# The last layer's output product: split into f16 halves instead of four-byte ones, with g scaled by a power of two

## Chip, cores and metric

The kernel runs on one core of a Trainium2 chip. The metric is the device time of one execution in microseconds (us): 507.54 us is the median of three runs before the change (507.1 to 508.44).

## What is computed

Attention with sigmoid weights, a soft mixture of experts, and a last layer on its output:

```python
scores = q @ k.T / sqrt(64) - log(448)               # 4 batches x 12 heads, 448 tokens, head size 64
x = (sigmoid(scores) @ v) -> (1792, 768)
x = moe(x, phi, w1, w2)                              # 32 slots, 8 experts
h = x @ w_in                                         # 768 -> 2048
g = h * cos(h)
out = g @ w_out                                      # 2048 -> 768
```

The mixture ends in a product with 32 slots, so the kernel folds it into the last layer: m = slot_out @ w_in has 32 rows only, and h is the product of m and the tokens' combine weights.

## The kernel before

The change lies in the last layer, from about 250 us on. The 1792 tokens are four blocks t of 448, d_ff = 2048 is 16 chunks f of 128, and the 768 outputs are 6 tiles o of 128. A **unit** u is a pair (t, f). For each unit TensorE makes h (`hidden`, L1199: one product of 128x128 and 128x448); ScalarE and VectorE make g = h cos(h) from it in five passes of 448 elements (`scaled`, `rounded`, `centred`, `sined`, `product`, L1177 to L1193); and TensorE adds w_out[f].T @ g to six accumulators (`out_tile`, L1234). There are eight accumulation banks: six hold the accumulators of the current block, two the h of the units to come. A **stretch** is a run of units of one block; at its end the six accumulators are emptied (`evict`, L1256 to L1262) into SBUF, and either go out or are added to a later stretch of that block.

The first four units (`PLAIN`) multiply four-byte floats as they are, two records on TensorE for each output tile. The other sixty are **split**: `upper` (L1208, ScalarE) rounds g to fp32r as gh, `lower` (L1212, VectorE) makes gl = g - gh, and each output tile is three products, gh with wh, gh with wl, gl with wh. wh and wl are made likewise of w_out by `wo_hi` (L1120, ScalarE) and `wo_lo` (L1123, VectorE). w_out arrives as 64-bit floats in six buffers; `wo_abs` and `wo_steps` (`narrow`, L264 to L271) make 32-bit floats of a chunk, one pass on ScalarE and three on VectorE, one of them a shift (L267). A buffer is loaded again as soon as `wo_lo` has read it.

The order of the units sets when chunks are needed:

```python
SOME, PLAIN = 6, 4
units = [(t, f) for t in range(2) for f in range(SOME)] + [(2, f) for f in range(NF)]
units += [(t, f) for t in range(2) for f in range(SOME, NF)]
units += [(t, f) for t in range(3, B) for f in range(NF)]
```

The first few instructions are written by hand (`m_hi` to `out_half`). From there a planner (`Plan`, filled by `schedule`) sets the order on every engine: each step has an engine, a cost and its predecessors, TensorE's steps get their due times from the sum of the costs ahead of them, the others from who needs them, and at each moment the ready step that is due first is issued. Each engine then runs its instructions in that order. A unit's h may be made once unit u-2's product is done (two banks), and `upper` waits for the last tile of unit u-2 (two buffers for gh and gl). m itself comes from a last set of products; `m_split_lo` (L1157) finishes it, and the units from 3 on read parts of it that arrive by DMA.

Of the kernel before, what the change touches and what calls it, by code (L numbers as in the profile page):

```python
# [9 lines left out]
F16 = mybir.dt.float16  # L10
F32 = mybir.dt.float32
F32R = mybir.dt.float32r
U32 = mybir.dt.uint32
AF = mybir.ActivationFunctionType
ALU = mybir.AluOpType
AX = mybir.AxisListType
PSUM = bass.MemoryType.PSUM

B, H, S, D = 4, 12, 448, 64
HP = H // 2  # L20
NP = B * HP
NT, DM = B * S, H * D
# [3 lines left out]
P = 128  # L26
NT_B = S // 32
KD = DM // P
NF = DFF // P
# [9 lines left out]
LATE = 1  # L39

CV = 512
F64_SCALE = 2.0 ** -112

LOG2E = 1.0 / math.log(2.0)
# [114 lines left out]
def fused(ctx: ExitStack, tc: tile.TileContext, qk, vv, phi, w1, w2, w_in, w_out, out):  # L159
    nc = tc.nc  # L160
# [6 lines left out]
    ident = const.tile([P, P], F32, name="ident")  # L167
# [141 lines left out]
    with ExitStack() as at:  # L309
# [58 lines left out]
        top, bottom = rows = slice(0, D), slice(D, P)  # L368
# [311 lines left out]

        pieces = [(c, n) for c in range(KD) for n in range(DFF // CV)]
        narrowing = {}

        def narrow_piece(p):
            c, n = pieces[p]
            k, o = divmod(n * CV, 1024)
            w = wt["wi", 0, c, k].bitcast(U32).rearrange("p a (f t) -> p (a f) t", t=2)
# [217 lines left out]
    ps_h = ctx.enter_context(reuse("ps_h", bufs=2, space=PSUM))  # L905
# [23 lines left out]
    m_ps, MC = {}, 4 * P  # L929
# [27 lines left out]
    with ExitStack() as ex:  # L957
# [3 lines left out]
        with tc.manual_schedule():  # L961
# [99 lines left out]
            for c in range(0, F // P - 2, 2):  # L1061
                w2_rows(1, c)
                if c == 0:
                    ps = [choose(0, k) for k in range(2)]
# [12 lines left out]
            ps = choose(1, 0)  # L1077
# [12 lines left out]

    wctx.close()
    wop = ctx.enter_context(reuse("wop", bufs=1, side="right"))
    wl = wop.tile([P, NF, DM], F32R, name="wl")
    wh = wop.tile([P, NF, DM], F32R, name="wh")
    more_wo.append(ctx.enter_context(reuse("more_wo", bufs=1, side="right")))
    stg = ctx.enter_context(reuse("stg", bufs=3))
    gp = ctx.enter_context(reuse("gp", bufs=2))
    m4 = places["m4"].tile([P, DFF], F32R, tag="w", name="m4")
# [3 lines left out]
    def whole(f):  # L1102

        return wo[f][:, :, 1].bitcast(F32)

    steps = {}
# [10 lines left out]
            steps[f].pop(0)()  # L1117

    def wo_hi(f):
        nc.scalar.copy(wh[:, f], whole(f))  # L1120

    def wo_lo(f):
        nc.vector.tensor_sub(wl[:, f], whole(f), wh[:, f].bitcast(F32))  # L1123
        load_wo(f + WO_SLOTS)

    def m_parts(f):
# [14 lines left out]
    mh, ml = [ring[:, (12 + k) * S:(12 + k) * S + 3 * P] for k in range(2)]  # L1141
# [16 lines left out]
        spread([0], (2, 3))  # L1158
        spread(range(1, 4), range(4))

    SOME, PLAIN = 6, 4
    units = [(t, f) for t in range(2) for f in range(SOME)] + [(2, f) for f in range(NF)]
    units += [(t, f) for t in range(2) for f in range(SOME, NF)]
    units += [(t, f) for t in range(3, B) for f in range(NF)]
    gs, acc, sums = {}, {}, {}

    spare = [raw_wo[k].rearrange("p m t -> p (m t)")[:, 2 * DM:2 * DM + S].bitcast(F32) for k in range(A_SLOTS)]

    def buf(k):
        return ring[:, k * S:(k + 1) * S]  # L1170

    hs, tmp = {}, {}
# [17 lines left out]

    def times(u, cols):
        ph, tn, g = tmp[u]
        nc.vector.tensor_mul(g[:, cols], hs[u][:, cols], tn[:, cols])  # L1193

    def hidden(u):
        t, f = units[u]
        ps = ps_h.tile([P, 512], F32, tag="h", name=f"h{u}")
        h = hs[u] = ps[:, 0:S]
        nc.tensor.matmul(h, m4[:, f * P:(f + 1) * P], ct4[:, t * S:(t + 1) * S], start=True, stop=True)  # L1199
        tmp[u] = [spare[k] if u == 0 else buf(3 * (u % 4) + k) for k in range(3)]  # L1200

    def product(u):
        times(u, whole_s)
        gs[u] = [tmp.pop(u)[2]]

    def upper(u):
        gs[u].append(gp.tile([P, S], F32R, tag="gh", name=f"gh{u}"))
        nc.scalar.copy(gs[u][1], gs[u][0])  # L1208

    def lower(u):  # L1210
        gs[u].append(gp.tile([P, S], F32R, tag="gl", name=f"gl{u}"))
        nc.vector.tensor_sub(gs[u][2], gs[u][0], gs[u][1].bitcast(F32))  # L1212

    def out_half(cols, os):

# [8 lines left out]
    def out_tile(u, o):  # L1224
        t, f = units[u]
        if begins(u):
            acc[o] = bank(o, f"o{u}_{o}")
        ps, cols = acc[o][:, 0:S], slice(o * P, (o + 1) * P)
        if u < PLAIN:
            terms = [(whole(f), gs[u][0])]  # L1230
        else:
            terms = [(wh[:, f], gs[u][1]), (wl[:, f], gs[u][1]), (wh[:, f], gs[u][2])]
        for n, (w, g) in enumerate(terms):
            nc.tensor.matmul(  # L1234
                ps, w[:, cols], g, start=begins(u) and n == 0, stop=ends(u) and n == len(terms) - 1
            )
# [7 lines left out]
    def adds(u):  # L1244
        return units[u][0] < 2 and units[u][1] == NF - 1

    def by_vector(u, o):
        return adds(u) or units[u][1] == NF - 1 and o % 2 == 1

    def evict(u, o):  # L1250
        t, f = units[u]
        ps = acc[o][:, 0:S]
        copy = nc.vector.tensor_copy if by_vector(u, o) else nc.scalar.copy
        if f < NF - 1:
            sums[t, o] = buf(18 + o) if t == 0 else buf(24 + o) if o < 3 else spare[o - 3]
            copy(sums[t, o], ps)  # L1256
            return
        res = buf(12 + o)
        if adds(u):
            nc.vector.tensor_add(res, ps, sums[t, o])  # L1260
        else:
            copy(res, ps)  # L1262
        nc.sync.dma_start(out=out[o * P:(o + 1) * P, t * S:(t + 1) * S], in_=res)

    plan = Plan()
    Op = plan.add

    def schedule():

        n_units = len(units)  # L1270
        mul, hid, tile, freed, raw_done = {}, {}, {}, {}, {}
        parts, his, los = {}, {}, {}

        def load(f):
            if f < WO_SLOTS:
                return -9.0, ()
            return -9.0, (landed[f],)

        landed = {}

        def chunk(f):
            if f in parts:
                return
            if f > 2:
                a = Op("act", .82, lambda: wo_abs(f), [landed.get(f), parts.get(f - 3)])
            else:
                a = None
            for c in (.6, 1., .9):
                a = Op("dve", c, lambda: wo_steps(f), [a])
            parts[f] = a  # L1290

        def split(f):
            if f in los:
                return
            if f > 1:
                chunk(f)
            his[f] = Op("act", .8, lambda: wo_hi(f), [parts.get(f)])
            los[f] = Op("dve", .9, lambda: wo_lo(f), [his[f], tile.get((f, NO - 1)) if f < PLAIN else None])
            if f + WO_SLOTS < NF:
                landed[f + WO_SLOTS] = Op("sp", 1.95, lambda: None, [los[f]])  # L1300

        def wave_ops(u):
            if u > 2:
                hid[u] = Op("pe", .2, lambda: hidden(u), [mul.get(u - 2), hid.get(u - 1)])
            a = Op("act", .57, lambda: scaled(u, whole_s), [hid.get(u), downs.get(u - 4) or tile.get((u - 4, NO - 1))])
            a = Op("act", .57, lambda: rounded(u, whole_s), [a])
            a = Op("dve", .54, lambda: centred(u, whole_s), [a])
            a = Op("act", .5, lambda: sined(u, whole_s), [a])
            mul[u] = Op("dve", .54, lambda: product(u), [a])
            if u >= PLAIN:  # L1310
                g = Op("act", .5, lambda: upper(u), [mul[u], tile.get((u - 2, NO - 1))])
                ups[u] = g
                downs[u] = Op("dve", .54, lambda: lower(u), [g])

        ups, downs = {}, {}

        def tiles(u, os):
            t, f = units[u]
            for o in os:
                need = [last_tile[0]]  # L1320
                if o == 0:
                    need += [mul.get(u)] if u < PLAIN else [ups[u], downs[u], his[f], los[f]]
                    need += [parts.get(f)]
                if begins(u):
                    need.append(freed.get(o))
                tile[u, o] = last_tile[0] = Op(
                    "pe", .694 if u < PLAIN else .602, lambda o=o: out_tile(u, o), need
                )
                if ends(u):
                    freed[o] = Op(  # L1330
                        "dve" if by_vector(u, o) else "act", .55, lambda o=o: evict(u, o), [tile[u, o]]
                    )

        last_tile = [None]
        wave_ops(2)
        wave_ops(3)
        for u in range(1, n_units):
            f = units[u][1]
            if u > 1:
                if u < PLAIN:  # L1340
                    chunk(f)
                else:
                    split(f)
            tiles(u, range(2))
            if u + 3 < n_units:
                wave_ops(u + 3)
            tiles(u, range(2, NO))
# [99 lines left out]
```

## Time and profile before

| | |
|---|---|
| median of three runs | 507.54 us (507.1 to 508.44) |
| span of the profiled execution | 506.7 us; the execution's own time is not shown |
| TensorE products busy | 481.8 us (95%), 4560 |
| TensorE weight loads busy | 349.3 us (69%), 4560 |
| VectorE busy | 325.5 us (64%), 655 |
| ScalarE busy | 292.3 us (58%), 508 |
| mean granted TensorE clock | 0.993 |

Busy times are averages over stages with different limits: attention runs to 150 us, the experts' weights stream in until about 245 us, and the last layer takes the rest. Matmuls are pipelined, so a record of 0.36 us does not mean that the next product starts 0.36 us later; the distance between starts is the pace.

### The profile page before, as it was taken

Reading aid. Unit: us, or ns where it says so; the run is one execution under the profiler, and the core shown is the slowest. Engines: PE = TensorE matmul, PEld = TensorE weight load, DVE = VectorE, ACT = ScalarE, POOL = GpSimd, SP = SyncE. Lnnn points to the kernel's source line nnn. Section 1 sums busy time; section 2 is a strip of 40 time slices with the busy share of each in tenths; the row PEclk is TensorE's granted clock in tenths of the full one; section 3 lists DMA queues with packets and bytes.
Section 4 is the critical chain, followed back from the end, with each engine's and each line's share of the span. In section 5 each row is a group of like instructions: output and inputs, shape, how many; then the busy total and the mean of one; then the engine's idle time right before and its main releaser. Section 6 shows DMA issues by size and latency. Waiting matters only on the chain.

```text
span 506.7 us, 11038 instructions
## 1 busy us (share of the span) xinstructions
PE 481.8 (95%) x4560; PEld 349.3 (69%) x4560; DVE 325.5 (64%) x655; ACT 292.3 (58%) x508; POOL 0.7 (0%) x7
## 2 busy tenths in 40 slices
PE   8998989999999998677999999999999999999997
PEld 5665556565565323222567999999999899899996
DVE  4898879999975063000689899996644654654442
ACT  5887858877861002000679889865655545555552
POOL 0000000000000000000000000000000000000000
PEclk9999999999999998999999999999999999999999
DMA  7999979979839999999824633000210110020003
GB/s 254 393 314 329 295 254 358 328 225 361 278 116 378 403 417 415 413 415 389 354 56 149 232 124 125 1 2 0 76 35 1 45 64 1 26 85 0 1 0 110
DMA packets 33442, 99.12 MB, mean 196 GB/s; under 512 B 3568, under 2 KB 17520, under 8 KB 33392
## 3 DMA queue, kind: packets, MB, share of 16 engines
q1 hardware_dynamic: 33392, 98.42, 53.3%
q8 instruction: 36, 0.59, 0.5%
q14 instruction: 14, 0.11, 0.1%
HBM read 92.11 MB, written 5.51 MB: 193 GB/s over the span
## 4 chain that ended last, share of the span: by engine, by line
PE 66%; DMA 18%; DVE 11%; ACT 2%; issue 2%; SPq 0%; DVEq 0%; ACTq 0%
PE o L1234 45%; DMA w<-in_w 14%; PE av L414 6%; PE sc L395 4%; DMA raw<-in_qk 3%; PE h L1199 3%; DVE lo L376 2%; PE sl L633 2%; DVE wi L268 1%; DVE hi L373 1%; PE idle L474 1%; DVE xt L424 1%; DMA wi<-in_w_in 1%; PE o L1219 1%; PE m L945 1%
## 5 line engine op out<-in xcount | busy, mean ns | idle before, releaser
L1234 PE MATMUL o<-gh,wh 128*128 128x448 f32 x360 | 132.3, 367 | 0.4 <-DVE wi L1260 0.4
L1234 PE MATMUL o<-gl,wh 128*128 128x448 f32 x360 | 131.5, 365 | 0.0
L1234 PE MATMUL o<-gh,wl 128*128 128x448 f32 x360 | 131.5, 365 | 0.0
L403 ACT ACTIVATE a<-sc,bias_s 128x896 f32<-128x896 f32 x72 | 71.1, 1006 | 27.1 <-PE sc L395 19.6
L1234 PEld LDWEIGHTS o<-gh,wh 128*128 128x128 f32 x360 | 67.6, 188 | 7.3 <-issue 1.3
L1234 PEld LDWEIGHTS o<-gh,wl 128*128 128x128 f32 x360 | 67.6, 188 | 5.4 <-issue 0.2
L1234 PEld LDWEIGHTS o<-gl,wh 128*128 128x128 f32 x360 | 67.6, 188 | 5.3
L1212 DVE TENSOR_TENSOR gl<-wi,gh 128x448 fp32r<-128x448 f32 x60 | 37.4, 623 | 41.1 <-ACT gh L1208 37.9
L1208 ACT CAST gh<-wi 128x448 fp32r<-128x448 f32 x60 | 34.1, 568 | 51.2 <-PE o L1234 49.3
L414 PE MATMUL av<-a,v 128*64 128x224 f32 x576 | 60.4, 357 | 2.6 <-DVE xt L424 1.5
L414 PEld LDWEIGHTS av<-a,v 128*64 128x64 f32 x576 | 39.0, 137 | 23.2 <-issue 4.1
L1193 DVE TENSOR_TENSOR wi<-h,wi 128x448 f32<-128x448 f32 x63 | 39.2, 622 | 21.5 <-ACT wi L1189 21.1
L1189 ACT ACTIVATE wi<-wi 128x448 f32<-128x448 f32 x63 | 36.4, 578 | 24.8 <-DVE wi L1184 24.7
L1184 DVE SCALAR_TENSOR_TENSOR wi<-wi 128x448 f32<-128x448 f32 x63 | 39.2, 622 | 15.3 <-ACT wi L1180 15.3
L1008 PE MATMUL so<-w,zone 128*32 128x256 f32 (+1 forms) x256 | 34.2, 517 | 9.8 <-DMA w<-in_w 9.8
L395 PEld LDWEIGHTS <-hi 64*64 64x64 f16 x768 | 25.0, 107 | 21.9 <-issue 13.5
L1180 ACT ACTIVATE wi<-wi 128x448 f32<-128x448 f32 x63 | 36.5, 580 | 1.7
L395 PE MATMUL sc<-hi 64*64 64x448 f16 (+1 forms) x384 | 34.0, 342 | 2.3 <-ACT a L403 1.6
L1177 ACT ACTIVATE wi<-h 128x448 f32<-128x448 f32 x63 | 33.9, 538 | 3.8 <-PE h L1199 3.6
L395 PE MATMUL sc<-hi,lo 64*64 64x448 f16 (+1 forms) x384 | 33.3, 330 | 0.0
L395 PE MATMUL sc<-lo,hi 64*64 64x448 f16 (+1 forms) x384 | 33.1, 329 | 0.1
L1008 PEld LDWEIGHTS so<-w,zone 128*32 128x32 f32 x256 | 9.7, 114 | 31.4 <-DMA w<-in_w 20.3
(160 smaller groups left out, 552.3 us busy)
## 6 DMA issues: line engine op xcount, KB each, us to landing
w<-in_w SPq DMA_DIRECT2D x28, 768.0 KB, 15.1
w<-in_w SPq DMA_DIRECT2D x30, 512.0 KB, 5.7
wi<-in_w_in SPq DMA_DIRECT2D x24, 512.0 KB, 7.3
wo<-in_w_out SPq DMA_DIRECT2D x16, 768.0 KB, 7.0
w<-in_w SPq DMA_DIRECT2D x11, 1024.0 KB, 9.5
raw<-in_qk SPq DMA_DIRECT2D x48, 224.0 KB, 5.1
v<-in_vv SPq DMA_DIRECT2D x24, 224.0 KB, 4.9
out_t<-wi SPq DMA_DIRECT2D x24, 224.0 KB, 2.0
```

The source lines that it names most:

```text
L395: nc.tensor.matmul(ps[to, j, 0:cols.stop - cols.start], keys[at, first:first + D], q[at, cols], **flags)
L403: nc.scalar.activation(a, ps, AF.Sigmoid, bias=bias_s, scale=qk_scale)
L414: nc.tensor.matmul(av[i][rows[j], k, 0:S // 2], v32[i][at, vc:vc + D], a[at, j, sides[k] if g < 3 else slice(0, S // 2)], start=g == 0, st ...
L1008: nc.tensor.matmul(e2[g, k][j * NS:(j + 1) * NS, 0:n], h1[g][:, c, j * NS:(j + 1) * NS], w(j), start=c == 0, stop=c == F // P - 1,)
L1177: nc.scalar.activation(tmp[u][0][:, cols], hs[u][:, cols], AF.Copy, bias=0.25, scale=inv2pi)
L1180: nc.scalar.activation(tmp[u][1][:, cols], tmp[u][0][:, cols], AF.Copy, bias=magic)
L1184: nc.vector.scalar_tensor_tensor(out=ph[:, cols], in0=tn[:, cols], scalar=-magic, in1=ph[:, cols], op0=ALU.add, op1=ALU.subtract)
L1189: nc.scalar.activation(tmp[u][1][:, cols], tmp[u][0][:, cols], AF.Sin, scale=-2.0 * math.pi)
L1193: nc.vector.tensor_mul(g[:, cols], hs[u][:, cols], tn[:, cols])
L1208: nc.scalar.copy(gs[u][1], gs[u][0])
L1212: nc.vector.tensor_sub(gs[u][2], gs[u][0], gs[u][1].bitcast(F32))
L1234: nc.tensor.matmul(ps, w[:, cols], g, start=begins(u) and n == 0, stop=ends(u) and n == len(terms) - 1)
```

## The change

It stores wh, wl, gh and gl in f16 instead of fp32r. So that the halves fit f16's range, w_out is multiplied by 8 as it is split, and g by a power of two, which is worked out on the chip from the largest magnitude of m (`bound`, `bound_row`, `powers`, `powers_all`, `keep_powers`: two maxima along rows and three small steps on VectorE, a product with the identity on TensorE that lays the 128 maxima into one row, five small steps on VectorE, a product that hands the two powers to all partitions, and a copy). Evictions of scaled units multiply by the inverse. The plain units stay unscaled, so block 0's first stretch now ends after them.

```diff
-    wl = wop.tile([P, NF, DM], F32R, name="wl")
-    wh = wop.tile([P, NF, DM], F32R, name="wh")
+    wl = wop.tile([P, NF, DM], F16, name="wl")
+    wh = wop.tile([P, NF, DM], F16, name="wh")
...
     def wo_hi(f):
-        nc.scalar.copy(wh[:, f], whole(f))
+        nc.scalar.activation(wh[:, f], whole(f), AF.Copy, scale=W_SCALE)
 
     def wo_lo(f):
-        nc.vector.tensor_sub(wl[:, f], whole(f), wh[:, f].bitcast(F32))
+        nc.vector.scalar_tensor_tensor(
+            out=wl[:, f], in0=whole(f), scalar=W_SCALE, in1=wh[:, f], op0=ALU.mult, op1=ALU.subtract
+        )
...
-    SOME, PLAIN = 6, 4
-    units = [(t, f) for t in range(2) for f in range(SOME)] + [(2, f) for f in range(NF)]
-    units += [(t, f) for t in range(2) for f in range(SOME, NF)]
+    SOME, PLAIN = (4, 6), 4
+    units = [(t, f) for t in range(2) for f in range(SOME[t])] + [(2, f) for f in range(NF)]
+    units += [(t, f) for t in range(2) for f in range(SOME[t], NF)]
...
     def times(u, cols):
         ph, tn, g = tmp[u]
-        nc.vector.tensor_mul(g[:, cols], hs[u][:, cols], tn[:, cols])
+        if u < PLAIN:
+            nc.vector.tensor_mul(g[:, cols], hs[u][:, cols], tn[:, cols])
+            return
+        nc.vector.scalar_tensor_tensor(
+            out=g[:, cols], in0=hs[u][:, cols], scalar=g_scale, in1=tn[:, cols], op0=ALU.mult, op1=ALU.mult
+        )
...
     def upper(u):
-        gs[u].append(gp.tile([P, S], F32R, tag="gh", name=f"gh{u}"))
+        gs[u].append(gp.tile([P, S], F16, tag="gh", name=f"gh{u}"))
...
     def lower(u):
-        gs[u].append(gp.tile([P, S], F32R, tag="gl", name=f"gl{u}"))
-        nc.vector.tensor_sub(gs[u][2], gs[u][0], gs[u][1].bitcast(F32))
+        gs[u].append(gp.tile([P, S], F16, tag="gl", name=f"gl{u}"))
+        nc.vector.tensor_sub(gs[u][2], gs[u][0], gs[u][1])
...
     def evict(u, o):
...
+        if adds(u):
+            nc.vector.scalar_tensor_tensor(
+                out=res, in0=ps, scalar=g_back, in1=sums[t, o], op0=ALU.mult, op1=ALU.add
+            )
+        elif by_vector(u, o):
+            nc.vector.tensor_scalar_mul(res, ps, g_back)
+        elif u < PLAIN:
+            nc.scalar.copy(res, ps)
+        else:
+            nc.scalar.activation(res, ps, AF.Copy, scale=g_back)
...
-                hid[u] = Op("pe", .2, lambda: hidden(u), [mul.get(u - 2), hid.get(u - 1)])
+                hid[u] = Op("pe", .2, lambda: hidden(u), [mul.get(u - 2), hid.get(u - 1), scaling.get(u)])
...
-            mul[u] = Op("dve", .54, lambda: product(u), [a])
+            mul[u] = Op("dve", .54, lambda: product(u), [a, x if u >= PLAIN else None])
...
-                    "pe", .694 if u < PLAIN else .602, lambda o=o: out_tile(u, o), need
+                    "pe", .694 if u < PLAIN else .567, lambda o=o: out_tile(u, o), need
...
+        x, scaling = None, {}
+        for eng, cost, step in (
+            ("dve", 1.2, bound), ("pe", .25, bound_row), ("dve", .6, powers), ("pe", .1, powers_all),
+            ("dve", .1, keep_powers),
+        ):
+            x = Op(eng, cost, step, [x])
+        scaling[3] = x
```

How this moves instructions shows at three places. The first is TensorE's order at unit 1, the second of the plain units (`h2` is the hidden product of unit 2, `o0_3` an accumulator of block 0's first stretch, tile 3). Before:

```order
L1199 MATMUL h2_3738<-ct4_3288,m4_3601 128x448
L1219 MATMUL o0_5_3740<-wo2_3527,wo0_3523 128x224 x2
L1199 MATMUL h3_3745<-ct4_3288,m4_3601 128x448
L1234 MATMUL o0_0_3679<-wi_64,wo1_3525 128x448
L1234 MATMUL o0_1_3681<-wi_64,wo1_3525 128x448
L1234 MATMUL o0_2_3683<-wi_64,wo1_3525 128x448
```

And in the change:

```order
L1208 MATMUL h2_3740<-ct4_3288,m4_3601 128x448
L1228 MATMUL o0_5_3742<-wo2_3527,wo0_3523 128x224 x2
L1243 MATMUL o0_0_3681<-wi_64,wo1_3525 128x448
L1294 MATMUL scale_3754<-ident_58,scales_3602 1x128
L1243 MATMUL o0_1_3683<-wi_64,wo1_3525 128x448
L1308 MATMUL scale_3754<-row_3603 128x2
L1243 MATMUL o0_2_3685<-wi_64,wo1_3525 128x448
L1208 MATMUL h3_3770<-ct4_3288,m4_3601 128x448
```

The hidden product of unit 3 has moved behind three tiles of unit 1, and the two small products stand between those tiles.

The second place is VectorE's order from the end of the split of m on (`wf2`, `wo2` are chunk 2 of w_out on its way to 32 bits). Before:

```order
L1157 TENSOR_TENSOR wi_64<-m2_3553,wi_64 128x384
L1193 TENSOR_TENSOR wi_64<-h1_3668,wi_64 128x448
L267 TENSOR_SCALAR wf2_3696<-wf2_3696 128x768
L1184 SCALAR_TENSOR_TENSOR wi_64<-wi_64 128x448
L268 SCALAR_TENSOR_TENSOR wf2_3696<-wo2_3527,wf2_3696 128x768
```

In the change, from the product of unit 1 on:

```order
L1198 TENSOR_TENSOR wi_64<-h1_3670,wi_64 128x448
L1285 TENSOR_REDUCE scales_3602<-m4_3601 128x1
L1288 TENSOR_REDUCE scales_3602<-wi_64 128x1
L1289 TENSOR_TENSOR scales_3602<-scales_3602 128x1
L1290 MEMSET row_3603 1x128
L269 TENSOR_SCALAR wf2_3698<-wf2_3698 128x768
L1299 TENSOR_REDUCE row_3603<-scale_3754 1x1
L1300 TENSOR_SCALAR row_3603<-row_3603 1x1
L1301 TENSOR_SCALAR row_3603<-row_3603 1x1
L1302 TENSOR_SCALAR row_3603<-row_3603 1x1
L1305 TENSOR_SCALAR row_3603<-row_3603 1x1
L1188 SCALAR_TENSOR_TENSOR wi_64<-wi_64 128x448
```

Nine of the ten small steps stand in a block there, with one shift of chunk 2 between them; the tenth, the copy of the powers, follows the last row.

The third place is TensorE's order where the split units begin, at unit 4. Before:

```order
L1234 MATMUL o0_5_3740<-wi_64,wo3_3604 128x448
L1234 MATMUL o0_0_3679<-gh4_3806,wh_3591 128x448
L1234 MATMUL o0_0_3679<-gh4_3806,wl_3590 128x448
L1234 MATMUL o0_0_3679<-gl4_3813,wh_3591 128x448
L1234 MATMUL o0_1_3681<-gh4_3806,wh_3591 128x448
```

In the change:

```order
L1243 MATMUL o0_5_3742<-wi_64,wo3_3606 128x448
L1243 LDWEIGHTS wh_3591
L1243 MATMUL o4_0_3835<-gh4_3818,wh_3591 128x448
L1243 LDWEIGHTS wl_3590
L1243 MATMUL o4_0_3835<-gh4_3818,wl_3590 128x448
L1243 LDWEIGHTS wh_3591
L1243 MATMUL o4_0_3835<-gl4_3827,wh_3591 128x448
```

Each weight load is now an instruction of its own (1080 more on TensorE in all), and unit 4 begins a new accumulator, since it is block 1's first.

## Rows read from the trace of the kernel before

**Rows 1.** Busy us (instructions) by stretch; then PEclk, DMA share, GB/s.

```profile
300.00:350.00 50.00, 50.00 (x249) 46.33 (x248) 45.88 (x71) 40.02 (x72) 0.00 (x0) 1.00 0.13 44
350.00:400.00 50.00, 50.00 (x248) 46.10 (x247) 24.73 (x41) 28.50 (x54) 0.00 (x0) 1.00 0.08 28
```

**Rows 2.** Chain that ended last, in order: start us, us, what.

```profile
251.05 1.34 PE o L1219 x6
...
257.34 3.01 PE o L1234 x8
...
268.47 4.22 PE o L1234 x14
...
342.00 0.20 PE h L1199
342.20 3.65 PE o L1234 x18
...
490.43 12.78 PE o L1234 x63
```

**Rows 3.** Weight loads by form: busy us, mean ns; idle before.

```profile
L1234 PEld LDWEIGHTS o<-gh,wl 128*128 128x128 f32 x360 | 67.6, 188 | 5.4 <-issue 0.2
...
L395 PEld LDWEIGHTS <-lo 64*64 64x64 f16 x384 | 11.7, 107 | 3.1 <-issue 0.2
...
L414 PEld LDWEIGHTS av<-one,v 64*64 64x64 f32 x192 | 6.5, 133 | 4.0 <-ACT one L403 1.4 <-issue 0.3
...
L1219 PEld LDWEIGHTS o<-wo,wo 128*128 128x128 f32 x24 | 4.4, 196 | 1.3 <-DVE wf L268 0.6 <-issue 0.6
```

**Rows 4.** Timeline of TensorE in the attention: three sets start between these.

```profile
105.72 0.36 PE L395 MATMUL sc<-hi 64*64 64x448 f16 x4
...
106.29 0.27 PE L395 MATMUL sc<-hi 64*64 64x224 f16 x4
```

**Rows 5.** VectorE and ScalarE groups by form: busy us, mean ns; idle before.

```profile
L1212 DVE TENSOR_TENSOR gl<-wi,gh 128x448 fp32r<-128x448 f32 x60 | 37.4, 623 | 41.1 <-ACT gh L1208 37.9 <-PE o L1234 3.2
L376 DVE TENSOR_TENSOR lo<-raw,hi 128x448 f16<-128x448 f32 x48 | 29.1, 613 | 0.5
...
L616 DVE SCALAR_TENSOR_TENSOR s_acc<-s_acc,al,sl 128x192 f32<-128x192 f32 x4 | 1.4, 407 | 0.1
...
L549 DVE SCALAR_TENSOR_TENSOR e<-e,x 128x128 f32<-128x128 f32 x5 | 1.4, 281 | 0.0
...
L506 DVE TENSOR_REDUCE mb<-l 128x1 f32<-128x128 f32 x3 | 0.8, 278 | 0.0
...
L510 DVE TENSOR_REDUCE mb<-four 32x1 f32<-32x4 f32 x3 | 0.4, 145 | 0.1
...
L1208 ACT CAST gh<-wi 128x448 fp32r<-128x448 f32 x60 | 34.1, 568 | 51.2 <-PE o L1234 49.3 <-DVE wi L1184 1.1 <-DVE wi L1193 0.7
...
L381 ACT CAST hi<-raw 128x448 f16<-128x448 f32 x1 | 0.6, 564 | 1.8 <-DMA raw<-in_qk 1.8
```

**Rows 6.** Timeline of VectorE as the last layer begins.

```profile
256.04 0.55 DVE L267 TENSOR_SCALAR wf<-wf 128x768 uint32<-128x768 uint32 x1
257.60 0.62 DVE L1184 SCALAR_TENSOR_TENSOR wi<-wi 128x448 f32<-128x448 f32 x1 [1.01 <-ACT wi L1180]
...
263.08 0.62 DVE L1184 SCALAR_TENSOR_TENSOR wi<-wi 128x448 f32<-128x448 f32 x1
263.62 0.95 DVE L271 SCALAR_TENSOR_TENSOR wo<-wo,wf 128x768 uint32<-128x768 uint32 x1
264.48 0.55 DVE L267 TENSOR_SCALAR wf<-wf 128x768 uint32<-128x768 uint32 x1
265.07 0.96 DVE L268 SCALAR_TENSOR_TENSOR wf<-wo,wf 128x768 uint32<-128x768 uint32 x1
```

**Rows 7.** Timeline of a hand-over from TensorE to VectorE.

```profile
143.42 0.38 PE L611 MATMUL zs<-run_z,fold 128*128 128x1 f32 x2
...
143.84 0.16 DVE L612 COPY run_z<-zs 128x1 f32<-128x1 f32 x1 [0.47 <-PE zs L611]
```

**Rows 8.** Waits, 270 to 345 us: us in total, times, longest us.

```profile
ACT gh L1208 <- PE o L1234: 8.7, 13, 1.1
```

More of the change, by code (lines that the diff above doesn't have):

```diff
@@ L41 @@
 CV = 512
+W_SCALE, G_BITS = 8.0, 14
 F64_SCALE = 2.0 ** -112
@@ L1252, in evict @@
         ps = acc[o][:, 0:S]
-        copy = nc.vector.tensor_copy if by_vector(u, o) else nc.scalar.copy
+        res = buf(12 + o)
         if f < NF - 1:
-            sums[t, o] = buf(18 + o) if t == 0 else buf(24 + o) if o < 3 else spare[o - 3]
-            copy(sums[t, o], ps)
-            return
[L1258 to L1262, printed above, removed]
-        nc.sync.dma_start(out=out[o * P:(o + 1) * P, t * S:(t + 1) * S], in_=res)
+            res = sums[t, o] = buf(18 + o) if t == 0 else buf(24 + o) if o < 3 else spare[o - 3]
@@ new lines, in evict @@
+        if adds(u):
[8 more added lines that the diff above has]
+            nc.scalar.activation(res, ps, AF.Copy, scale=g_back)
+        if f < NF - 1:
+            return
+        nc.sync.dma_start(out=out[o * P:(o + 1) * P, t * S:(t + 1) * S], in_=res)
@@ new lines, in fused, with bound @@
+    scales = gp.tile([P, 4], F32, tag="scales", name="scales", bufs=1)
+    g_scale, g_back = scales[:, 0:1], scales[:, 1:2]
+    row = gp.tile([1, P + 4], F32, tag="row", name="row", bufs=1)
+    def bound():
+        nc.vector.tensor_reduce(
+            out=scales[:, 2:3], in_=m4[:, 0:MC].bitcast(F32), axis=AX.X, op=ALU.max, apply_absolute_value=True
+        )
+        nc.vector.tensor_reduce(out=scales[:, 3:4], in_=mh, axis=AX.X, op=ALU.max, apply_absolute_value=True)
+        nc.vector.tensor_max(scales[:, 2:3], scales[:, 2:3], scales[:, 3:4])
+        nc.vector.memset(row[:, 0:P], 1.0)
@@ new lines, in bound_row, with powers @@
+    def bound_row():
+        steps["scale"] = ps_h.tile([P, 512], F32, tag="h", name="scale")
+        nc.tensor.matmul(steps["scale"][0:1, 0:P], scales[:, 2:3], ident, start=True, stop=True)
+    def powers():
+        top, (s, back) = row[:, P:P + 1], (row[:, P + k:P + k + 1] for k in (2, 3))
+        nc.vector.tensor_reduce(out=top, in_=steps["scale"][0:1, 0:P], axis=AX.X, op=ALU.max)
+        nc.vector.tensor_scalar_max(top, top, 2.0 ** -100)
+        nc.vector.tensor_single_scalar(top.bitcast(U32), top.bitcast(U32), 0x7F800000, op=ALU.bitwise_and)
+        nc.vector.tensor_scalar(
+            s.bitcast(U32), top.bitcast(U32), -1.0, float((2 * 127 + G_BITS) << 23), op0=ALU.mult, op1=ALU.add
+        )
+        nc.vector.tensor_scalar_mul(back, top, 2.0 ** -G_BITS / W_SCALE)
@@ L1265, in fused, with powers_all, keep_powers @@
+    def powers_all():
+        nc.tensor.matmul(
+            steps["scale"][:, P:P + 2], row[:, 0:P], row[:, P + 2:P + 4], start=True, stop=True
+        )
+    def keep_powers():
+        nc.vector.tensor_copy(scales[:, 0:2], steps.pop("scale")[:, P:P + 2])
     plan = Plan()
```

## Prediction

> **What bounds the kernel now.** I read the busy time by stretch first, then the chain of waits, then the groups of TensorE and of VectorE, and last the timeline where the change puts something new. [...] A unit of the last layer is one hidden product of 0.20 us and 18 output products in 3.65 us, 0.203 us each, and the last unpaused run, 63 products in 12.78 us, has the same pace [rows 2]. Nothing but that pace and the number of products (60 units of 18, 1080) sets the end.
>
> What sets 0.203 us? The plain units, in four-byte floats, leave records of 0.376 us for 448 columns (8 in 3.01) and of 0.223 us for 224 columns (6 in 1.34) [rows 2]. Half the columns should take half, 0.188; the 224-column products are held up by their weight loads, of 0.196 us [rows 3]. The split products load weights of the same shape in 0.188 us [rows 3] and start 0.203 apart, again the load plus some 0.015 to 0.03. So the pace of 0.203 is the pace of loading 128 columns of four-byte weights, and the streaming of 448 columns would allow less.
>
> **The change, part by part.**
> *The split products in f16.* No f16 product on the whole array is in this trace. The nearest are the scores: sets of four 64x64 f16 products with 448 columns, each set filling the array, every one with its own weight load. Three sets take 0.57 us from start to start [rows 4], 0.190 a set. Their weight load of 64 f16 columns takes 0.107 us against 0.133 us for 64 four-byte columns [rows 3]. Four-byte loads grow from 0.133 to 0.188 when the columns double, a factor of 1.41; by the same factor an f16 load of 128 columns is an estimated 0.15 us, under 0.19. Then the load hides and the stream sets the pace. I take 0.190; the ends are 0.187 (0.57 us is read to 0.01, so 0.56 over three sets) and 0.203 (no change). Saved: 1080 x (0.2028 - 0.190) = **13.8 us**. That each load is now an instruction of its own I cost at nothing: it runs under the product before it, as the loads of the scores do [rows 4]; without that cover it would cost its 0.15 us 1080 times, which no row suggests.
>
> [...]
>
> *The work on VectorE and ScalarE.* Exact twins are in the trace: f16 written from four-byte minus f16 takes 0.613 us against 0.623 us now, and ScalarE's cast to f16 0.564 against 0.568 [rows 5]. So the halves of g cost nothing more or less. The products with a per-partition scale are nearest to the slot sums, 0.407 us for 192 elements [rows 5]; a straight line between 0.281 us at 128 elements and 0.623 us at 448 [rows 5] puts 0.35 us there, so the scale costs between nothing and 0.06 us. I take nothing, since the slot sums also read two more dimensions; the other end is 1.3 us of VectorE over the 21 units in which it is nearly full.
>
> *The search for the power of two.* It is new on the path, since h of unit 3 and everything behind it on TensorE's queue wait for it. VectorE reaches it at 256.04 us [rows 6]. Two maxima (448 elements reduced cost about as much as other 448-element work, here 512 and 384: together 1.1 us), a small maximum and a memset (0.145 us each, the row of a 32x4 reduction [rows 5]) end near 257.4 us. TensorE begins unit 1 at 257.34 - 0.20 = 257.14 us [rows 2], as hidden product 3 no longer stands before it, and its first tile of 0.75 us ends at 257.9: the first small product, some 0.2 us, finds its input ready. From a small product's start to VectorE's first work on it takes 0.42 us [rows 7]; a reduction of 128 elements 0.28 us [rows 5] and four steps of 0.145 us follow, to 259.2 us. TensorE has done its second tile at 258.85 us and stands some 0.5 us for the second small product, which takes 0.2 us. Added: 0.2 + 0.5 + 0.2 = **0.9 us**. The ends are 0.4 us (no standing) and 3 us (two hand-overs of 0.42 and nine small steps at 0.28 us each, less the tile of 0.75 beside them, with the two products). On VectorE the chain costs some 2.3 us and 1 us of waiting, of which 1.0 us falls into a wait that stands there today [rows 6].
>
> *The order of the units.* Block 0 stops after its four plain units, so block 2, for which chunks 6 to 15 must be made, comes at unit 10 and not at unit 12. The number of stretches, and of evictions between them, stays: 6 tiles each to ScalarE or VectorE. Evictions behind scaled units get a multiplication in the same pass. I cost them at 0.3 us in all, since 5 tiles of cover shrink from 3.05 to 2.85 us.
>
> *Whether VectorE keeps up.* This is the cover of the 13.8 us in its first third. Counted in the order, from the split of m to the last low half whose weights are new (unit 25's in both), VectorE issues 72 instructions of 448 elements, 14 shifts and 43 others of 768 elements, and the ten small ones; at issue distances of 0.54, 0.59 and 0.86 us [rows 6] and 3.3 us for the chain this is 38.9 + 8.3 + 37.0 + 3.3 = 87.5 us, from 256.0 to 343.5 us. The run of 14 records from 268.47 us is 8 plain ones and unit 4's first 6 [rows 2], so TensorE begins unit 4 at 268.47 + 8 x 0.376 + 0.9 = 272.4 us and, at the new pace of 18 x 0.190 + 0.203 = 3.62 us a unit, unit 25 at 348.5 us: 5 us are left, and nearly 10 would have been at the old pace. The waits that VectorE has now are mostly for ScalarE's upper half, which itself waits for TensorE, 8.7 us in 75 us [rows 8], so they are the slack and not a need. The tightest place is between the low halves of units 10 and 11, where three 448s, two shifts and three 768s (5.4 us) must fit; after unit 8 ends, the upper half, the low half and this sum take 0.57 + 0.62 + 5.4 = 6.6 us, and two units give 7.2 us. It holds, by little; I put 0.4 us for places where it does not.
>
> **The sum.** -13.8 + 0.9 + 0.3 + 0.4 = -12.2 us. The trace's span is 506.7 us, so the span forecast is 494.5 us. The profiled execution's own time isn't shown; the median of the runs, 507.54 us, lies 0.84 us over the span, and I carry that over: **495.3 us**. Below 0.3% (1.5 us) I call it the same, about what a measurement of this kernel can tell from none.
>
> **The rivals.**
> *VectorE becomes the bound of the first third.* For it: 92% busy, and only 5 us left. Against: the waits it has now are slack. If its instructions there took 10% longer, 87.5 us would become 96.3, past unit 25's start by 4 us; with waits on ScalarE on top by 6. Time 497 to 501 us.
> *The pace does not fall, and the change is slower.* If what holds 0.203 us is not the width of the weights, but the change of weights under a whole-array product as such, the 13.8 us go and the 0.9 + 0.3 + 0.4 us stay: 509.1 us. The point from which it decides: a pace over 0.2013 us, as 1080 times the remaining 0.0015 is 1.6. [...] Against: the 224-column products, the two 64-column loads and the scores.
> *The stream alone sets the pace, and the search hides.* At 0.187 us the products save 17.1 us, and with 0.4 us for the search and nothing for the rest the time is 490.8 us.
>
> **How the numbers follow.** The forecast's case 0.74 (492.5 to 497), VectorE as bound 0.11, pace unchanged 0.07, the fast end 0.08. The range of 491.5 to 499.5 us holds the first and most of the second and fourth, some 0.84. Faster by over 0.3%: all cases but the unchanged pace, 0.93, less 0.02 for a pace just under 0.2013, which would come out the same; so 0.91, 0.02, and 0.07 for slower.
>
> **What would show it.** Right: the split products start 0.19 us apart, with weight loads well under that; a unit with its hidden product takes 3.6 us; a gap of half a microsecond on TensorE near 259 us before the second small product; no gap over 0.5 us up to 350 us. Wrong: products 0.2 us apart; weight loads of f16 still near 0.19; TensorE waiting for low halves of g or of w_out between 295 and 350 us.

## The result and the profile after

The changed kernel takes 494.12 us (median of four runs, 493.34 to 494.95) against 507.32 us for the kernel before, run beside it (506.9 to 508.44): a ratio of 0.9728, 95% interval 0.9689 to 0.9767. The forecast was 495.3 us. The profiled execution's span went from 506.7 to 492.7 us, 14.0 us less.

The same two stretches as [rows 1], in the changed kernel (busy us and instructions of TensorE, its weight loads, VectorE, ScalarE, GpSimd; granted clock; DMA share; GB/s):

```profile
300.00:350.00 50.00, 50.00 (x264) 25.86 (x263) 48.32 (x75) 41.28 (x72) 0.00 (x0) 1.00 0.14 48
350.00:400.00 50.00, 50.00 (x263) 25.65 (x261) 30.04 (x49) 29.33 (x57) 0.00 (x0) 1.00 0.15 56
```

TensorE is still busy throughout, at the same granted clock of 1.00, and issues 264 products in 50 us where it issued 249. Its weight loads fell from 46 us to 26. VectorE went from 46 to 48 of 50 us: it keeps up, by little.

The chain that ended last, which answers to [rows 2] (start us, us, what):

```profile
256.49 0.75 PE o L1243 x2
257.24 0.31 PE scale L1294 x2
257.55 0.96 PE o L1243 x2
258.51 0.00 issue
258.51 0.38 PE scale L1308 x2
258.88 0.96 PE o L1243 x2
...
268.93 4.14 PE o L1243 x14
...
320.14 0.20 PE h L1208
320.34 3.42 PE o L1243 x18
...
429.16 3.49 PE o L1243 x18
...
436.28 0.34 PE h L1208
...
477.02 11.95 PE o L1243 x63
```

A unit is 0.20 + 3.42 us now, 3.62 from one to the next where it was 3.85, and the last 63 products take 11.95 us, 0.1897 each, where they took 12.78. The whole chain from 256 us on is TensorE; no step of VectorE or ScalarE stands in it until the last eviction. Where the 14.0 us of span come from, by this chain and that of before (h of unit 3, then unit 1, began at 257.14 us there, the split units at 268.47 + 8 x 0.376 = 271.48, their last product ended at 503.21):

| stretch | before | after | difference |
|---|---|---|---|
| up to unit 1 (or h3) | 257.14 | 256.49 | -0.65 |
| units 1 to 3, with the search | 14.34 | 15.45 | +1.11 |
| the sixty split units | 231.73 | 217.02 | -14.71 |
| last eviction and output | 3.49 | 3.74 | +0.25 |

The first line is not put down to the change: in the experiments the last layer began between 254.0 and 258.5 us. So the experiments below are also compared by the length of the **last layer** alone, from the start of unit 1 (of h3, where that comes first) to the end of the last product: 246.07 us before, 232.47 us after. Experiments 1 to 5 and 8 are one run each, the others four to ten.

Groups of instructions by form in the changed kernel (busy us, mean ns; idle before):

```profile
L1200 DVE SCALAR_TENSOR_TENSOR wi<-h,scales,wi 128x448 f32<-128x448 f32 x60 | 40.9, 681 | 13.6 <-ACT wi L1193 12.3
L1221 DVE TENSOR_TENSOR gl<-wi,gh 128x448 f16<-128x448 f32 x60 | 37.4, 623 | 32.7 <-ACT gh L1217 32.2
L1243 PEld LDWEIGHTS <-wl 128*128 128x128 f16 x360 | 35.3, 98 | 28.1 <-issue 0.6
L1217 ACT CAST gh<-wi 128x448 f16<-128x448 f32 x60 | 33.7, 562 | 41.9 <-PE o L1243 31.1 <-DVE wi L1200 10.0 <-DVE wo L273 0.8
L1274 ACT ACTIVATE wi<-o,scales 128x448 f32<-128x448 f32 x9 | 5.6, 632 | 4.2 <-PE o L1243 4.2
```

And two groups of the kernel before that they answer to, besides those of [rows 3, 5]:

```profile
L1193 DVE TENSOR_TENSOR wi<-h,wi 128x448 f32<-128x448 f32 x63 | 39.2, 622 | 21.5 <-ACT wi L1189 21.1
L1256 ACT COPY wi<-o 128x448 f32<-128x448 f32 x9 | 4.7, 534 | 0.3 <-PE o L1234 0.2
```

The halves of g cost what they did (623 and 562 ns, where they took 623 and 568). The product with the scale rose from 622 to 681 ns, and an eviction on ScalarE from 534 to 632. A weight load is recorded with 98 ns against 188.

### The profile page after: what moved, and what is told of

It is laid out like the page before. It is cut to its first block, busy times and chain, and to the rows that moved or that the text cites. A ratio compares the mean times of both kernels' runs of the same rounds, so it can differ in the third digit from the quotient of the medians.

```text
span 492.7 us, 11063 instructions
## 1 busy us (share of the span) xinstructions
PE 467.9 (95%) x4564; PEld 248.7 (50%) x4564; DVE 330.4 (67%) x665; ACT 291.4 (59%) x508; POOL 0.7 (0%) x7
## 4 chain that ended last, share of the span: by engine, by line
PE 71%; DMA 17%; DVE 8%; ACT 2%; issue 1%; SPq 0%; ACTq 0%
PE o L1243 45%; DMA w<-in_w 13%; PE av L416 9%; PE sc L397 5%; PE h L1208 3%; DMA v<-in_vv 2%; PE h L974 2%; PE sl L635 2%; DMA raw<-in_qk 2%; DVE lo L378 1%; ACT a L405 1%; PE o L1228 1%; DVE xt L426 1%; PE m L947 1%; DVE hi L375 1%
## 5 line engine op out<-in xcount | busy, mean ns | idle before, releaser
L1243 PE MATMUL o<-gh,wh 128*128 128x448 f16 x360 | 127.4, 354 | 0.0
L1243 PE MATMUL o<-gl,wh 128*128 128x448 f16 x360 | 126.9, 352 | 0.0
L1243 PE MATMUL o<-gh,wl 128*128 128x448 f16 x360 | 126.9, 352 | 0.0
L1243 PEld LDWEIGHTS <-wh 128*128 128x128 f16 x720 | 70.3, 98 | 71.8 <-issue 11.1
L1221 DVE TENSOR_TENSOR gl<-wi,gh 128x448 f16<-128x448 f32 x60 | 37.4, 623 | 32.7 <-ACT gh L1217 32.2
L1217 ACT CAST gh<-wi 128x448 f16<-128x448 f32 x60 | 33.7, 562 | 41.9 <-PE o L1243 31.1
L1200 DVE SCALAR_TENSOR_TENSOR wi<-h,scales,wi 128x448 f32<-128x448 f32 x60 | 40.9, 681 | 13.6 <-ACT wi L1193 12.3
L1243 PEld LDWEIGHTS <-wl 128*128 128x128 f16 x360 | 35.3, 98 | 28.1 <-issue 0.6
L1010 PE MATMUL so<-w,zone 128*32 128x256 f32 (+1 forms) x256 | 36.2, 534 | 9.6 <-DMA w<-in_w 9.5
L1208 PE MATMUL h<-ct,m 128*128 128x448 f32 x64 | 33.6, 525 | 0.3 <-DVE m L1143 0.3
```

The lines of the kernel that those rows point to most:

```text
L1010: nc.tensor.matmul(e2[g, k][j * NS:(j + 1) * NS, 0:n], h1[g][:, c, j * NS:(j + 1) * NS], w(j), start=c == 0, stop=c == F // P - 1,)
L1200: nc.vector.scalar_tensor_tensor(out=g[:, cols], in0=hs[u][:, cols], scalar=g_scale, in1=tn[:, cols], op0=ALU.mult, op1=ALU.mult)
L1221: nc.vector.tensor_sub(gs[u][2], gs[u][0], gs[u][1])
L1243: nc.tensor.matmul(ps, w[:, cols], g, start=begins(u) and n == 0, stop=ends(u) and n == len(terms) - 1)
```

## The experiments

**1 and 2. Does the weight load set the pace?** My reading was that the load of 128 four-byte columns holds the products 0.203 us apart. If so, half the streamed columns change nothing in the kernel before.

```diff
+            half = first if n == 1 else whole_s
             nc.tensor.matmul(
-                ps, w[:, cols], g, start=begins(u) and n == 0, ...
+                ps[:, half], w[:, cols], g[:, half], start=begins(u) and n == 0, ...
```

`first` is the first 224 of the 448 columns, `n == 1` the product of gh and wl, the second of a tile's three. On the kernel before:

> The kernel before, in which the second of the three products of a split tile (wl with gh) streams 224 columns instead of 448; the other half of that product is left out. If the load of the next weights sets the pace of the fp32r products (my theory), the half product still takes some 0.2 us until the next one starts, and the time stays within 1 us of the kernel before, 507 us. If the streaming of the columns sets it (rival), 360 products lose half of 0.203 us, 36 us, and the time is near 471 us, less where VectorE then becomes the bound.

And the same edit on the changed kernel:

> The changed kernel with the same edit: the product of wl with gh streams 224 columns, half of it is left out. My theory: with f16 the load (0.098 us) is short and the stream of 448 columns is the pace, so the half product takes about 0.11 us (load plus 0.015) instead of 0.19, 0.48 us less per unit in 60 units, 29 us at most; in the first third VectorE lets only some 5 us of 10 through, so 494 falls to 470 to 474 us. If something else held the f16 products at 0.19 (the change of weights as such), the time stays at 494 us.

Measured: 487.66 us on the kernel before (507.96 beside it) and 474.83 on the changed one. The chain of the first, early in the last layer:

```profile
270.48 3.10 PE o L1235 x18
273.78 3.04 PE o L1235 x18
276.81 7.46 DMA wo<-in_w_out
```

And the last run of the second:

```profile
458.88 9.99 PE o L1244 x63
```

18 four-byte products took 3.04 to 3.10 us where TensorE had no gap, not 3.65: my reading falls. (Its last 63 took 11.00 us, 0.19 more than at 0.515 a tile. One tile among them waits for VectorE's last low half:

```profile
478.93 0.19 PEld L1235 LDWEIGHTS o<-gl,wh 128*128 128x128 f32 x1 [0.21 <-DVE gl L1212]
```

That accounts for it.) The time did not come down to the rival's either, since other work took over as soon as TensorE was faster: the chain stands 7.46 us for a transfer of w_out, and later for VectorE and ScalarE. In f16 a tile takes 9.99 / 21 = 0.4757 us, so the short product 0.4757 - 2 x 0.1897 = 0.096, half of 0.19 and less than the 0.11 expected: its time went with its columns, with nothing added for the load.

**3. Half the weights.** The same product in the kernel before with 64 of its 128 weight columns, streaming all 448, so that half of that term's outputs are left out:

```diff
+            n_w = 64 if n == 1 else P
             nc.tensor.matmul(
-                ps, w[:, cols], g, start=begins(u) and n == 0, ...
+                ps[0:n_w], w[:, o * P:o * P + n_w], g, start=begins(u) and n == 0, ...
```

> The kernel before, in which the product of wl with gh is made for 64 of the 128 rows of the output tile: its weights have 64 columns, and half of that product is left out; its stream keeps 448 columns. My theory: the load of 64 columns takes 0.137 us and hides under the product before it, which then lasts 0.190 us; the next load is full again. Saved: 360 x 0.0128 = 4.6 us, 502.7 us. If the four-byte stream sets 0.203 us (rival), nothing changes, 507.3 us.

Measured: 509.68 us. The load's group, and the end of the chain:

```profile
L1235 PEld LDWEIGHTS o<-gh,wl 128*64 128x64 f32 x360 | 48.3, 134 | 6.1 <-issue 0.2
```

```profile
419.97 3.63 PE o L1235 x18
...
482.89 3.72 PE o L1235 x18
491.37 13.03 PE o L1235 x63
```

The recorded load shrank from 188 to 134 ns, the pace did not: 3.63 us a unit in two stretches, 3.72 in the others, against 3.65; by my reading it would have been 3.57. So the length of the load is not what the products wait for. Why some stretches are even slower by 2% stays open.

**4. Four-byte products with 112 and with 256 columns.** The same edit as in the first experiment, with another slice. First 112 columns, to part three readings of the 0.203 us:

> The kernel before with the product of gh and wl streaming 112 columns instead of 448 (the other two as they are), so that a part of the output is left out. It tells apart what the 0.203 us of a four-byte product consist of, now that half-width weights (13.03 us for 63 products) did not lower them and half the columns (11.00 us for 63) did. Three readings, each for the 18 products of a unit where TensorE has no gap, which with 224 columns took 3.08 to 3.10 us and with 448 take 3.65 us. (a) A fixed cost of some 0.015 us on top of streaming at the f16 kernel's pace (0.1897 us for 448 columns, 0.0475 for 112): a tile takes 2 x 0.2028 + 0.0475 + 0.015 = 0.468 us, 18 products 2.81 us. (b) Slower streaming in proportion to the columns, 0.2028/448 = 0.000453 us each: 2 x 0.2028 + 0.051 = 0.456 us a tile, 2.74 us for 18. (c) A floor by the weight load, which the half-column run puts at 0.10 us or less: 2 x 0.2028 + 0.10 = 0.506 us a tile, 3.03 us for 18. The whole time is no measure here, since ScalarE, VectorE and the transfers bounded much of the half-column run (487.7 us): 478 to 487 us by any of the three, with the last 63 products at 9.83 us by (a), 9.58 by (b), 10.6 by (c).

Measured: 485.73 us, and in the chain:

```profile
273.44 3.08 PE o L1235 x18
276.73 3.08 PE o L1235 x18
```

No less than with 224 columns. The short product stands on a floor, 3.08 / 6 - 2 x 0.2028 = 0.107 us, the third reading. The records around one short product say whose floor it is. The load that starts with it is followed by the next load 0.10 us later, though each is recorded with 0.19; elsewhere loads start 0.2 us apart:

```profile
476.27 0.19 PEld L1235 LDWEIGHTS o<-gl,wh 128*128 128x128 f32 x1
476.37 0.19 PEld L1235 LDWEIGHTS o<-gh,wh 128*128 128x128 f32 x1
```

I put the floor down to the load; no run shortens the load at 112 columns. The equal time also took the force out of the half-column run as a measure of streaming, since it stood on the same floor. So a size above it:

> The kernel before with the product of gh and wl streaming 256 columns (a part of the output is left out). With 112 columns the 18 products of a unit took 3.08 us, no less than with 224 (3.08 to 3.10): both stand on a floor of 3.08/6 - 2 x 0.2028 = 0.107 us for the shortened product, which I take for the weight load behind it. So the half-column run said nothing of what the 0.203 us of a 448-column product consist of, beyond that it is not this floor. At 256 columns both readings that are left lie over the floor, where TensorE has no gap: (a) the f16 kernel's streaming (0.1897 at 448, 0.096 at 224, so 0.109 at 256) and a fixed 0.013 us: 2 x 0.2028 + 0.1225 = 0.528 us a tile, 3.17 us for 18; (b) slower streaming in proportion, 0.2028 x 256/448 = 0.116: 0.5215 us a tile, 3.13 us for 18. (c) If the shortened product still takes 0.107, 3.08. The whole time is no measure (ScalarE and VectorE bound much of it): some 487 to 489 us.

Measured: 485.65 us. The chain:

```profile
276.34 3.17 PE o L1235 x18
279.71 3.17 PE o L1235 x18
```

3.17 us, the first reading: 0.122 us for 256 columns, where f16 at its own pace would take 0.109, an estimate from its 0.096 us at 224 columns and 0.1897 at 448. At 448 columns the difference is 0.2028 - 0.1897 = 0.013: about the same at both sizes. The second reading would have given 3.13, and the six units without a gap here take 3.16 or 3.17. But both readings take the pace of the two full products as unchanged, which no run measures by itself, and in experiment 3 a unit moved by 0.07 us for a reason that stays open. So a fixed part is the better fit, and not proved. It did not shrink when one load in three had half its columns (experiment 3).

**5. The floor in f16.** 112 columns in the changed kernel:

> The changed kernel with the product of gh and wl streaming 112 columns (a part of the output is left out), for the floor of the f16 form. With 224 columns 18 products took 2.86 us, 0.096 for the shortened one, which is streaming. If a weight load of 128 f16 columns takes as long as one of four-byte columns (0.107), the floor would have shown at 224 columns already; it did not, so 0.107 is ruled out and the time here is between streaming (0.049 us: a tile 2 x 0.1897 + 0.049 = 0.428, 18 in 2.57 us) and a floor just under 0.096 (18 in 2.85 us). A load in proportion to the bytes (half of 0.107, so 0.054) gives 18 in 2.60 us. I expect 2.6. Whole time some 470 to 475 us, bounded by ScalarE and VectorE.

Measured: 471.82 us, and in the chain:

```profile
271.78 2.58 PE o L1244 x18
```

The short product takes 2.58 / 6 - 2 x 0.1897 = 0.051 us, and it has a load of 128 f16 columns behind it like every other. So such a load takes at most about 0.05 us of the array's time, though its record says 98 ns.

**6. The order alone.** The kernel before with the change's order of units and nothing else:

```diff
-    SOME, PLAIN = 6, 4
+    SOME, PLAIN = (4, 6), 4
```

(with the two lines of `units` as in the change.)

> The kernel before with the new order of the units alone: block 0's first stretch ends after the four plain units, the products stay in fp32r. I costed the order at nothing at the old pace: 507.3 us, within 1 us. If the order itself carries a part of the gain (rival: shorter stalls at the ends of the stretches, 1.2 us before and 0.45 us in the changed kernel), 0.8 us faster; if the earlier need of the chunks binds VectorE, TensorE shows waits for low halves before 350 us and the time is 1 to 3 us longer.

Measured: 507.32 us against 507.96, ratio 0.999 (0.9968 to 1.0011); the last layer takes 246.10 us, before 246.07. The order by itself gives and costs nothing.

**7. Without the search.** The changed kernel with the power of two as a constant, 2^23; it is the right one for these data only.

```diff
+GS = 2.0 ** 23
...
-    g_scale, g_back = scales[:, 0:1], scales[:, 1:2]
+    g_scale, g_back = GS, 1.0 / GS / W_SCALE
...
-        for eng, cost, step in (
-            ("dve", 1.2, bound), ("pe", .25, bound_row), ("dve", .6, powers), ("pe", .1, powers_all),
-            ("dve", .1, keep_powers),
-        ):
-            x = Op(eng, cost, step, [x])
-        scaling[3] = x
```

> The changed kernel with a constant power of two instead of the search: the maxima, the two small products, the five small steps and the copy are gone, and the scaled product and the evictions take their factor as an immediate. The search cost TensorE 1.1 us by the two traces (units 1 to 3 last 15.45 us instead of 14.34): I expect 493.0 us, 1.1 us under the changed kernel, with the scaled product back at 0.62 us instead of 0.68. Rival: the search is hidden anyway, since VectorE's 5 us of slack or another wait takes it over: no change, 494.1 us.

Measured: 492.04 us (490.77 to 495.63; 508.3 beside it), ratio 0.969 (0.9628 to 0.9751). The last layer takes 230.91 us, 1.56 less than in the change: units 1 to 3 take 14.34 us again, 1.11 less, and the other 0.45 us are the stretch ends, where the change's chain has two units of 3.49 and two hidden products of 0.34 to 0.35, and this one none. The group of the product:

```profile
L1201 DVE SCALAR_TENSOR_TENSOR wi<-h,wi 128x448 f32<-128x448 f32 x60 | 37.3, 621 | 14.9 <-ACT wi L1194 13.4
```

With the scale as a constant the same instruction takes 621 ns, not 681: the 0.06 us are the price of reading the scale from a tile, one per partition.

**8. More work for VectorE.** The changed kernel with `lower` issued twice for units 4 to 25:

```diff
-        nc.vector.tensor_sub(gs[u][2], gs[u][0], gs[u][1])
+        for _ in range(2 if u <= 25 else 1):
+            nc.vector.tensor_sub(gs[u][2], gs[u][0], gs[u][1])
```

> The changed kernel, in which VectorE makes the low half of g twice in units 4 to 25: 22 more instructions of 0.53 us, 11.7 us more on VectorE in the stretch where it is nearly full. My sum left it 5 us there, less 1.3 us for the scaled products at 0.68 instead of 0.62: TensorE loses 7 to 9 us, 501 to 503 us, in waits before unit 25. If VectorE has been the bound all along (rival), the whole 11.7 us appear, 506 us; if its slack is far larger than my sum, nothing does, 494 us.

Measured: 506.08 us; the last layer takes 241.86 us, 9.4 more. One of its stretches:

```profile
300.00:325.00 25.00, 23.24 (x119) 11.53 (x118) 24.76 (x41) 20.57 (x36) 0.00 (x0) 1.00 0.31 107
```

VectorE is full and TensorE has gaps. The 22 instructions more are 22 x 0.54 to 0.62 = 11.9 to 13.6 us of VectorE, of which 9.4 came out: the slack was 2.5 to 4.2 us. The 9.4 us are a little over the 7 to 9 expected. That the time itself came to the rival's 506 us is chance: the last layer also began 2 us later.

**9. A plain unit less.** The changed kernel with three plain units:

```diff
-    SOME, PLAIN = (4, 6), 4
+    SOME, PLAIN = (3, 6), 3
```

> The changed kernel with three plain units instead of four, so that the first split unit is unit 3: six tiles take 0.57 instead of 0.75 us on TensorE, 1.1 us saved, 493.0 us, if VectorE keeps up. The last new chunk is then needed 4.5 us earlier, and VectorE has only one unit's work (1.7 us) less until then: its slack shrinks by 2.8 us. If the slack is under that (rival), TensorE waits before unit 24 and the time is 494 to 496 us.

Measured: 495.26 us (494.75 to 496.24; 508.3 beside it), ratio 0.9738 (0.9683 to 0.9794), last layer 234.41 us, 1.94 more than in the change. The stretch in which most of it is lost, and its waits (engine, line, waited for: us in total, times, longest):

```profile
325.00:350.00 25.00, 23.36 (x120) 11.52 (x119) 24.36 (x37) 19.18 (x34) 0.00 (x0) 1.00 0.05 19
```

```profile
ACT gh L1217 <- DVE wi L1200: 3.4, 3, 1.7
PEld h L1208 <- DVE wi L1200: 1.8, 2, 1.0
```

TensorE and ScalarE wait for VectorE's scaled product there. (Some 0.6 us were lost before it, from 282 to 294 us, where ScalarE's evictions behind block 1's first stretch stand in the chain.) The rival holds: unit 3 is 1.1 us shorter on TensorE (18 x 0.190 instead of 12 x 0.376), more split work falls to VectorE earlier, and its slack doesn't hold that.

**10. The search spread further.** Two planner costs raised, so that the second small product stands behind one more tile:

```diff
-            ("dve", 1.2, bound), ("pe", .25, bound_row), ("dve", .6, powers), ("pe", .1, powers_all),
+            ("dve", 1.5, bound), ("pe", .25, bound_row), ("dve", 1.2, powers), ("pe", .1, powers_all),
```

> The changed kernel with two planner costs altered (the maxima 1.5 us instead of 1.2, the five steps on one row 1.2 instead of 0.6). The planner then puts the second small product behind one more tile of unit 1 (tile 0, small product, tiles 1 and 2, small product, tile 3, hidden products 3 and 4), nothing else being changed. Theory: of the 1.1 us by which units 1 to 3 take longer than before, 0.6 to 0.7 is TensorE standing for the second small product (waits of 0.7 and 0.6 us in the trace of the change, the first shown beside a tile still running); a tile of 0.75 us covers it. The last layer, from the start of unit 1 to the end of its last product 232.47 us in the changed kernel, takes 231.9 us, the time is 493.6 us, some 0.5 us lower. Rival: h of unit 3 comes later and with it VectorE's work, which has about 4 us of slack until unit 25; that slack shows no shortage, so nothing changes there, but the first units' g may come late: TensorE then waits before unit 3 or 4 by the same 0.5 us, the last layer stays at 232.5 us and the time at 494.1 us. Which of the two, the length of the last layer tells (the whole time varies by 2 us with the stage ahead).

Measured: 495.02 us (492.33 to 496.22, six runs; 507.92 beside them), ratio 0.9724 (0.9677 to 0.977); the last layer takes 489.52 - 256.65 = 232.87 us, 0.4 more than in the change. Its chain:

```profile
257.40 0.31 PE scale L1294 x2
257.71 1.71 PE o L1243 x4
259.42 0.32 PE scale L1308 x2
...
261.77 0.97 DVE wo L273
...
262.78 2.53 PE o L1243 x6
```

The four products behind the first small one still take 1.71 us instead of 4 x 0.376 = 1.50, so the 0.2 us that are lost behind a small product are no wait for VectorE. And chunk 2 of w_out (L273), which VectorE made later, became late instead: the six products at 262.78 are the first of unit 2. The rival is right in its direction, with another unit's input.

## Why the prediction held, and where it did not

**The pace, -13.8 us: right in size, wrong in its cause.** 0.190 was taken and 0.1897 measured. By whole units, 60 x (3.85 - 3.62) is 13.8 us of the 14.7 that the split units lost (by the last run, 1080 x (0.2028 - 0.1897), it is 14.1: in the change the first product behind a hidden one takes 0.20 us from start to start, at 320 us, the others 0.19). The scores [rows 4] gave the right number. But the step "the pace of 0.203 is the pace of loading 128 columns of four-byte weights" fell. Half the weight columns did not lower the pace (3.63 and 3.72 us a unit against 3.65, experiment 3), and the floor that I put down to the load is 0.107 us, far below it (experiment 4). What the runs show in its place: with 256 columns instead of 448 an fp32r product went from 0.2028 to 0.122 us (experiment 4), so the streaming sets most of the pace; and at 448 columns it takes 0.013 us more than the f16 one, at 256 about as much by the estimate of experiment 4. The change took away this small part. The error lay in reading the length of a load's record (0.188 us) as the time that it keeps the array: with 112 columns, loads recorded with 187 to 190 ns follow at 0.107 us. Which part of the four-byte form costs the 0.013 us, its wider operands or its being one instruction with its load, stays open; no run here separates them. The right size was no luck: it came from the f16 row itself, and did not use the wrong cause.

**The rival of an unchanged pace** was turned down by the right row, the scores, and by two wrong ones, the 224-column products and the 64-column loads, which do not show what sets the pace at 448 columns.

**The search, +0.9 us: measured +1.11, with other terms.** The first small product and VectorE in the changed kernel:

```profile
255.39 0.68 DVE L1285 TENSOR_REDUCE scales<-m 128x1 f32<-128x512 f32 x1
255.99 0.54 DVE L1288 TENSOR_REDUCE scales<-wi 128x1 f32<-128x384 f32 x1
...
257.17 0.38 PE L1294 MATMUL scale<-ident,scales 128*1 128x128 f32 x2
257.58 0.28 DVE L1299 TENSOR_REDUCE row<-scale 1x1 f32<-1x128 f32 x1 [0.32 <-PE scale L1294]
...
258.32 0.13 DVE L1305 TENSOR_SCALAR row<-row 1x1 f32<-1x1 f32 x1
```

VectorE's part came out as worked out: 0.41 us from the small product's start to the reduction (0.42 taken), 0.87 us for that and the four steps (0.86 taken). L1305 ended at 258.45, and TensorE's tile at 258.51: the standing of 0.5 us was not there, because TensorE itself was later. The small products took 0.31 and 0.38 us instead of 0.2 each, and the two products behind each took 0.96 us instead of 0.75: 0.69 + 0.42 = 1.11. So that 0.9 came near is in part luck: a term of 0.5 fell away, and others that were not in the sum came in for it. The expectation of experiment 10 misread this too: the trace lists a wait of 0.7 us of the second small product for L1305, but that wait ran beside a tile.

The records point to where the 0.2 us behind a small product go. In a row of tiles a weight load starts 0.18 us ahead of its product; behind the small product the two start together:

```profile
256.14 0.39 PEld L1243 LDWEIGHTS o<-wi,wo 128*128 128x128 f32 x2
256.32 0.92 PE L1243 MATMUL o<-wi,wo 128*128 128x448 f32 x2
...
257.48 0.31 PEld L1243 LDWEIGHTS o<-wi,wo 128*128 128x128 f32 x2 [0.22 <-issue]
257.48 1.03 PE L1243 MATMUL o<-wi,wo 128*128 128x448 f32 x2
```

So nothing covers the load there; that this is the whole of the 0.2 us, no run shows.

**VectorE's work: the scaled product costed at nothing, measured at its other end.** 0.06 us each, as between [rows 5]'s straight line and the slot sums; experiment 7 ties it to the scale read from a tile. It cost no time, since VectorE kept up: the forecast's 0.4 us for places where it does not were not needed, and no unit of the split took over 3.62 us up to 350 us. Of the 5 us of slack, 5 - 1.3 = 3.7 were left with the scaled product at its dearer end, and experiment 8 found 2.5 to 4.2. So this rival was close: one plain unit less brought it out (experiment 9).

**The order and the evictions, +0.3 us: the other way.** The order is worth nothing (experiment 6). Evictions grew by 0.06 to 0.10 us each, and the stretch ends show losses of 0.45 us in all. But the kernel before lost more there, some 1.3 us: in its chain two units take 8.15 instead of 7.70 us at 396 us, and 8.18 at 435 us, where TensorE waits for evictions on VectorE, and three others take 0.09 to 0.16 us more. Of that chain:

```profile
365.31 3.81 PE o L1234 x18
...
402.01 0.62 DVE wi L1260
402.77 1.45 PE o L1234 x6
```

The difference is the 0.9 us that the split units lost beyond the pace. The new order alone keeps these losses (experiment 6), and the changed kernel without the search has none (experiment 7). So they went with the f16 products, or with the tile's cost in the planner that was changed with them (0.602 to 0.567), and 0.45 us came back with the search; the first two were not tried apart.

**The sum.** -13.8 - 0.9 + 1.1 + 0.25 - 0.65 is the trace's -14.0, against -12.2 forecast. The 1.8 us between them are the stretch ends and evictions (0.95), the 0.4 that VectorE did not need and the 0.65 of the stage ahead, less 0.2 for the search. The last layer's own part is 13.6; the stage ahead varies by more than its 0.65.

## What to carry to other kernels

A weight load's record is not the time that it blocks the array (here 188 ns on record against at most 0.107 us, and 98 ns against at most 0.051); take the pace from the distance between starts, and test what sets it by shortening one operand at a time, the streamed columns and the weights apart, down to where a floor shows. A small product that is put between tiles also costs the products behind it: here 0.55 us each in all, where 0.2 had been counted. And when the bounding engine is made faster, count the next one's slack in instructions: here it was 2.5 to 4 us in some 90, and an edit that saved TensorE another 1.1 us lengthened the last layer by 1.9.

## What was not expected of the hardware

With fp32r operands the pace fits a fixed part: 0.2028 us at 448 columns and 0.122 at 256, against 0.1897 and an estimated 0.109 in f16, and no less than 0.107 at 112, where f16 went to 0.051. In f16 the time went nearly with the columns: 0.1897, 0.096 and 0.051 us for 448, 224 and 112, which is 0.42, 0.43 and 0.46 ns a column. The 0.1897 us held over 63 products in a row.
